# Gated linear attention and a SiLU feed-forward layer on one core: other places for a product block, two masks and a split in the written-out order of a step

## The chip, the cores and the metric

The kernel runs on one core of a Trainium2 chip. Times are device microseconds (us) of one execution. The kernel before was run 14 times: median 681.48 us, from 679.19 to 684.01.

The engines are named as in the profile: PE (TensorE, matrix products) with PEld (its weight loads), DVE (VectorE, elementwise work), ACT (ScalarE, functions from tables), POOL (GpSimd) and SP (SyncE). POOL and SP mostly issue transfers (DMA) here.

## The reference

For each of 4 batches and 8 heads, a state matrix of 48 x 48 complex numbers is carried over 768 positions. At each position it is multiplied by a complex gate, the outer product of k and v is added, and q reads it out. The result, laid out as 3072 tokens of 384 numbers, goes through a feed-forward layer.

```python
mag = np.sqrt(a_re * a_re + a_im * a_im)
scale = np.minimum(mag, 0.999) / (mag + 1e-06)
a_re_n, a_im_n = (a_re * scale, a_im * scale)
...
new_re = ar * S_re - ai * S_im
new_im = ar * S_im + ai * S_re
S_re, S_im = (new_re + kv, new_im)
y[:, :, t] = np.einsum('bhd,bhde->bhe', q[:, :, t], S_re)
...
h = x @ w_in
g = h * (1.0 / (1.0 + np.exp(-h)))
return (g @ w_out).astype(np.float32)
```

## The kernel before, in words

The sequence is cut into chunks of 128 positions: 6 chunks in each of 4 batches are 24 tiles, and two tiles (A and B, of two batches) make a pair p, of which there are 12 (p = 0 to 11). For each pair the kernel does the following.

- *Gates* (`gates_square` to `gates_angle`, lines 304 to 362): from a_re and a_im come l, the logarithm of the gate's size, and th, its angle in turns. ACT does squares, Ln, Exp and Arctan, DVE the sums and products between them. Each change of the set of functions is a table load on ACT (`table`, line 290).
- *Running sums*: th and l are summed over the positions of the chunk by a product with a triangle of ones (`phases`, `sums`). `in_two` (line 372) first splits the input into two parts on DVE. ACT then makes sines and cosines (`trig`, line 410) and exponentials (`decays`).
- *Attention*: DVE multiplies k and q by these (`rotated`) and transposes them in blocks (`turned`); the transfers of tile T on SP and POOL finish the transposition. PE makes the products of q and k (`weights`, line 496), DVE masks them (line 506), PE adds the part from the state (`output`) and makes the next state (`state`).
- *Feed-forward*: `hidden` (line 586) is one eighth of the first product for a pair: two columns of blocks of 256 tokens into the PSUM tile h, followed by SiLU on ACT into the tile g. `result` is one eighth of the second product. From pair 2 on it is done with seven block products for eight (`result_of_halves`, line 647), which needs sums of parts of g. `sums_of` (line 614) makes them on DVE into the tile gs: those of eighth jp+1 are made right behind the matmuls of eighth jp.

The pairs are staggered. After a start in which the pairs 0 to 2 are woven together, a loop over p = 3 to 12 does a *step* each: attention of pair p, feed-forward of pair p-1, and gates of pair p+1 (so gates are made in the steps p = 3 to 10, and the step p = 12 has feed-forward work alone). The order of all instructions in a step is written by hand, in the string `usual` (line 919), and each engine gets its instructions in that order. `step` (line 683) reads it token by token:

- h and r: one eighth of the first and of the second product; the eighths are counted in order, so that the n-th h and the n-th r of a step are called h1 to h8 and r1 to r8 below
- E: exponentials of pair p; kA, qA, kB, qB: `rotated`; tA, tB: `turned`; a0A, a1A, a0B, a1B: `weights` with its mask, for the heads 0 to 3 and 4 to 7; sA, sB: `state`; yA, yB: `output`
- D, L, F, G, th: the gates of pair p+1. D is squares, L the logarithm and what hangs on it, F the inverse of mag + th, G l, the ratio and the arctangent, th the side, the angle and the carried angle
- uA, uB and mA, mB: splits of th and of l; pA, pB: `phases`; lA, lB: `sums`; S: `trig`
- A and X: loads of gates for pair p+2, of k, q, v for pair p+1; c: the angles carried over

Where a token has nothing to do in a step it is left out. In the steps p = 11 and 12 every h and r is followed by `look` (line 722): a load of a part of the weights, and on DVE a smallest value of one that came earlier, for a check at the end.

Buffers that matter here: h has two PSUM buffers (pool `p_h`, line 114), shared by nothing else in the steps; the products of attention, the running sums and the states take turns in two more (pool `p_m`, line 113); gs has two buffers and g four.

Of the kernel before, what the change touches and what calls it, by code (L numbers as in the profile page):

```python
# [60 lines left out]
def kernel(  # L61
# [20 lines left out]
    B, H, S, D = q.shape  # L82
# [43 lines left out]
    A = [dict() for _ in range(NP)]  # L126
    X = {n: dict() for n in range(N)}
# [668 lines left out]
    with tc.manual_schedule(engines={mybir.EngineType.PE}):  # L796
# [104 lines left out]
        for n in (4, 5):  # L901
# [14 lines left out]
        both(trig, 3)  # L916
        startup_psum.close()
        late.append(fast.enter_context(tc.tile_pool(name="o_late", bufs=4, space=PSUM)))
    usual = ("c h E h kA qA h r tA D L kB F qB h r h tB r G h th uA uB A X a0A h a1A r sA h a0B yA "
             "r a1B sB r pA yB pB mA S mB r r lA lB")  # L920
    by_hand.append(True)
    with tc.manual_schedule():
        for p in range(3, NP + 1):
# [179 lines left out]
```

## Time and profile before

| what | value |
|---|---|
| median of 14 runs | 681.48 us |
| profiled execution, its own time | 681.21 us |
| its span, first to last instruction | 679.4 us |
| PE, PEld busy | 645.2, 572.8 us |
| DVE, ACT, POOL busy | 457.1, 345.5, 167.8 us |
| ACT table loads | 64, 1283 ns each |
| SiLU, one eighth | 596 ns |
| mask of `weights` | 685 ns |
| one step of the loop, between the same places of two passes | 52.02 us |

The profile is of one execution. Busy time is the union of an engine's instructions. A row of the timeline gives start and length in us, engine, line, operation, the tiles (out<-in), shapes and how many instructions it merges; in brackets stands how long the engine had been idle and what ended that wait. PE and PEld are one engine seen twice: weight loads run beside the matmul before them, and the ends of matmuls are modelled, so the distance between starts says more than a length.

### The profile page before, as it was taken

What the parts mean: (1) busy time and instruction counts of PE and PEld (TensorE: products, weight loads), DVE (VectorE), ACT (ScalarE), POOL (GpSimd) and SP (SyncE); (2) the same over time, 40 slices, a digit from 0 to 9 for tenths busy, and PEclk for the clock granted to TensorE, in tenths of its full rate; (3) what the DMA queues carried; (4) which work ended last, traced back from release to release, by engine and by line L of the source; (5) the groups of instructions that cost most, each with busy time, mean ns of one, the idle gap of its engine ahead of it and who ended that gap; (6) DMA issues with size and microseconds to landing.
All of it is one profiled execution on the core that took longest, in us unless ns stands there. A gap on an engine that the chain in (4) does not pass through costs nothing. (4 is left out here: it accounts for less than half of the span.)

```text
span 679.4 us, 11283 instructions
## 1 busy us (share of the span) xinstructions
PE 645.2 (95%) x4066; PEld 572.8 (84%) x4066; DVE 457.1 (67%) x979; ACT 345.5 (51%) x526; POOL 167.8 (25%) x256
## 2 busy tenths in 40 slices
PE   5788999999999999999999999999999999998995
PEld 3576777577989989989989989989989989997995
DVE  3786745939775875885784784784785784874532
ACT  7779543665942842752762761771780681510110
POOL 7473201340320320320330230240240240240000
PEclk8799999999999999999999999999999999998998
DMA  9968658281392382293184185184176164577630
GB/s 170 225 134 194 141 141 185 49 134 34 37 143 39 51 137 54 46 137 59 36 130 72 35 127 77 31 120 91 31 110 101 31 96 68 193 162 211 217 114 28
DMA packets 171488, 71.20 MB, mean 105 GB/s; under 512 B 155904, under 2 KB 160000, under 8 KB 171424
## 3 DMA queue, kind: packets, MB, share of 16 engines
q1 hardware_dynamic: 158304, 49.76, 36.8%
q0 software_dynamic: 8768, 15.92, 15.4%
q10 hardware_dynamic: 4352, 4.72, 2.0%
q8 instruction: 34, 0.56, 0.4%
q14 instruction: 30, 0.25, 0.1%
HBM read 48.86 MB, written 4.79 MB: 79 GB/s over the span
## 5 line engine op out<-in xcount | busy, mean ns | idle before, releaser
L591 PE MATMUL h<-xT,w 128*128 128x256 f32 x1152 | 260.9, 380 | 5.8 <-ACT g L295 4.7
L591 PEld LDWEIGHTS h<-xT,w 128*128 128x128 f32 x1152 | 215.9, 190 | 36.7 <-ACT g L295 7.1
L295 ACT ACTIVATE g<-h 128x512 f32<-128x512 f32 x96 | 55.5, 596 | 165.4 <-PE h L591 162.2
L492 POOL DMA_DIRECT2D T<-sq x120 | 78.5, 665 | 69.3 <-issue 59.3
L290 ACT ACT_TABLE_LOAD x64 | 82.1, 1283 | 2.5 <-PEq L1087 1.3
L663 PE MATMUL o<-w,gs 128*128 128x192 f32 x320 | 79.0, 329 | 0.0
L542 POOL DMA_DIRECT2D xT<-y x30 | 15.9, 535 | 216.2 <-ACT y L538 197.3
L506 DVE TENSOR_TENSOR w<-a,upto_r 128x512 f32<-128x512 f32 x48 | 32.0, 685 | 52.6 <-PE a L501 52.6
L663 PE MATMUL o<-w,g 128*128 128x192 f32 x320 | 66.8, 331 | 0.0
L663 PE MATMUL o<-wc,gs 128*128 128x192 f32 x320 | 65.1, 326 | 0.0
L534 ACT COPY xT<-y 128x384 f32<-128x384 f32 x20 | 9.6, 479 | 102.7 <-PE y L528 102.7
L663 PEld LDWEIGHTS o<-w,gs 128*128 128x128 f32 x320 | 56.0, 190 | 1.7 <-DVE gs L620 1.7
L663 PEld LDWEIGHTS o<-w,g 128*128 128x128 f32 x320 | 53.8, 190 | 3.5 <-issue 1.9
L620 DVE TENSOR_TENSOR gs<-g 128x128 f32<-128x128 f32 x160 | 38.9, 284 | 26.0 <-ACT g L295 14.6
L501 PEld LDWEIGHTS a<-T 96*128 96x128 f32 x384 | 49.3, 192 | 5.9 <-issue 2.8
L663 PEld LDWEIGHTS o<-wc,gs 128*128 128x128 f32 x320 | 54.2, 190 | 0.0
L440 POOL DMA_DIRECT2D decs<-ends x48 | 30.5, 642 | 92.3 <-DMA ends<-eq 91.3
L501 PE MATMUL a<-T 96*128 96x128 f32 x384 | 50.4, 276 | 2.7 <-DMA T<-sq 2.3
L633 PE MATMUL o<-w,g 128*128 128x384 f32 x128 | 42.6, 488 | 0.0
L663 PE MATMUL o<-wc,g 128*128 128x192 f32 x160 | 39.1, 326 | 0.0
L633 PEld LDWEIGHTS o<-w,g 128*128 128x128 f32 x128 | 24.2, 190 | 16.1 <-issue 0.2
L525 PE MATMUL y<-w,v 128*64 128x128 f32 x320 | 36.1, 288 | 0.0
(106 smaller groups left out, 953.2 us busy)
## 6 DMA issues: line engine op xcount, KB each, us to landing
T<-sq SPq DMA_DIRECT2D x120, 64.0 KB
T<-sq POOLq DMA_DIRECT2D x120, 64.0 KB, 4.3
raw<-in_moe_w_out_dram SPq DMA_DIRECT2D x16, 384.0 KB
small<-in_moe_w_in_dram SPq DMA_DIRECT2D x16, 384.0 KB
small<-in_moe_w_out_dram SPq DMA_DIRECT2D x16, 384.0 KB
raw<-in_moe_w_in_dram SPq DMA_DIRECT2D x24, 192.0 KB
out_dram<-ot ACTq DMA_DIRECT2D x23, 192.0 KB
q<-in_q_dram SPq DMA_DIRECT2D x18, 192.0 KB
```

The lines of the kernel that those rows point to most:

```text
L290: chain(nc.scalar.preload_act_table_set({"exp": "natural_log_exp_and_others", "trig": "trig_and_small", "silu": "silu_and_others"}[of]))
L295: chain(nc.scalar.activation(out=out, in_=in_, func=func, **kw))
L440: nc.gpsimd.dma_start(out=decs[a * D:(a + 1) * D, n], in_=ends[n].rearrange("(h d) -> d h", d=D))
L492: (nc.gpsimd if a % 2 else nc.sync).dma_start(out=to[ts(b, Q), :, a], in_=sq[ts(a, Q), b])
L501: nc.tensor.matmul(ps[:, h], lhsT=x["kT"][:, hh * HH + h], rhs=x["qT"][:, hh * HH + h], start=True, stop=True)
L506: nc.vector.tensor_tensor(out=x["w", hh], in0=ps, in1=upto.unsqueeze(1).to_broadcast([C, HH, C]), op=ALU.mult)
L525: nc.tensor.matmul(to, lhsT=v_[:, cols], rhs=x["w", h // HH][:, h % HH], start=True, stop=not carried)
L542: (nc.gpsimd if r and n >= EARLY else nc.sync).dma_start(out=xT[64 * r + D:64 * r + 64, dc], in_=y3[64 * r + third * dc:64 * r + third * ( ...
L591: nc.tensor.matmul(ps[:, ji], lhsT=w1[:, dc, ts(jp * 2 + ji, C)], rhs=A[p]["xT"][:, dc], start=(dc == 0), stop=(dc == ND - 1))
L620: nc.vector.tensor_tensor(out=t[:, i], in0=a, in1=b, op=op)
L633: nc.tensor.matmul(A[p]["o"][m].rearrange("p n c -> p (n c)"), lhsT=A[p]["g", jp][:, ji, ts(m, C)], rhs=w2[:, j], start=(j == 0), stop=(j ...
L663: nc.tensor.matmul(o[i], lhsT=a, rhs=b, start=(jp == 0 and i < 4), stop=(final and i in ((5, 3, 6, 2) if p == NP - 1 else (4, 5, 6, 2))))
```

## The change

Two lines of the string `usual` are written differently. h4 and its SiLU move from behind qB to ahead of L; qB and r2 stand between L and F; A, X and the first masked product a0A stand ahead of th, uA and uB; r7 stands ahead of mB. Nothing is added or removed.

```diff
-    usual = ("c h E h kA qA h r tA D L kB F qB h r h tB r G h th uA uB A X a0A h a1A r sA h a0B yA "
-             "r a1B sB r pA yB pB mA S mB r r lA lB")
+    usual = ("c h E h kA qA h r tA D kB h L qB r F h tB r G h A X a0A th uA uB h a1A r sA h a0B yA "
+             "r a1B sB r pA yB pB mA S r mB r lA lB")
```

## The prediction

> **What bounds the kernel now.** I read the page's rows of busy time and slices first, then the costliest groups with their releasers, then one loop pass (step p=7, 376.5 to 428.6 us) row by row.
>
> ```profile
> PE 645.2 (95%) x4066; PEld 572.8 (84%) x4066; DVE 457.1 (67%) x979; ACT 345.5 (51%) x526; POOL 167.8 (25%) x256
> PE   5788999999999999999999999999999999998995
> ...
> L591 PE MATMUL h<-xT,w 128*128 128x256 f32 x1152 | 260.9, 380 | 5.8 <-ACT g L295 4.7
> L591 PEld LDWEIGHTS h<-xT,w 128*128 128x128 f32 x1152 | 215.9, 190 | 36.7 <-ACT g L295 7.1
> ```
>
> TensorE is full in every slice from the fifth to the last but two. What can still be won is idle time of TensorE inside the steps, nothing else. The groups show one repeated hole: the weight loads of the first product (h) wait 7.1 us for a SiLU (g on ACT). In step p=7 the hole looks like this. The rows are "start, length, engine, line, operation"; the last fence shows the two other places that the change touches.
>
> ```profile
> 395.29 1.28 ACT L290 ACT_TABLE_LOAD   x1
> 396.58 1.09 ACT L295 ACTIVATE g<-h 128x512 f32<-128x512 f32 x2
> 397.69 1.28 ACT L290 ACT_TABLE_LOAD   x1
> ```
>
> ```profile
> 391.47 2.51 PEld L591 LDWEIGHTS h<-xT,w 128*128 128x128 f32 x12
> ...
> 396.01 0.35 PEld L663 LDWEIGHTS o<-w,gs 128*128 128x128 f32 x2
> 397.23 2.46 PEld L591 LDWEIGHTS h<-xT,w 128*128 128x128 f32 x12 [0.87 <-ACT g L295]
> ```
>
> I number the blocks of a step in TensorE's order: h1 h2 h3 r1 h4 r2 h5 r3 h6 a0A h7 a1A r4 sA h8 a0B yA r5 a1B sB r6 pA yB pB r7 r8 lA lB. The h tile has two PSUM buffers, so h6 needs the SiLU of h4. Its weight loads began at 386.60, and it was over by 389.6, but that SiLU stands in ACT's order behind L and F, and starts only at 396.58, after F's table load. It is done at 397.17; h6 starts at 397.23.
>
> ```profile
> 406.42 1.51 PEld L574 LDWEIGHTS s<-v,kr 128*96 128x96 f32 x16
> ...
> 426.64 0.30 PEld L663 LDWEIGHTS o<-w,gs 128*128 128x128 f32 x2 [0.21 <-DVE gs L620]
> ```
>
> ```profile
> 405.53 1.28 DVE L506 TENSOR_TENSOR w<-a,upto_r 128x512 f32<-128x512 f32 x2
> ...
> 426.31 0.48 DVE L620 TENSOR_TENSOR gs<-g 128x128 f32<-128x128 f32 x2
> ```
>
> Last block r8 waits 0.21 us for its sums gs, which DVE makes behind both l splits (mB). The masks of a0A and a1A run at 405.53, just ahead of sA, which takes the first mask's buffer.
>
> **What is not touched.** TensorE's order is the same before and after: only ACT and DVE tokens change places around h and r. SP and POOL issue in the same order too: A and X (4 and 6 loads on SP) pass th, uA and uB, which issue no DMA; r7 passes mB, which issues none; S's two stores stay behind tB and the y parts. There are 64 table loads before and after.
>
> **Part 1: h4 ahead of L** (steps p=3 to 10, eight of them, the ones with a next pair of gates). What a hole costs is read from first weight load to first weight load. An h after an r takes 2.54 us there (391.47 to 394.01), an r after an h 2.33. So r3 and h6 without a hole take 4.87; they take 399.71 - 394.01 = 5.70. Loss 0.83 us. The first step has 188.18 to 189.15 idle, 0.97, so 0.93; the other six, at 241, 293, 345, 449, 501 and 553, repeat the 0.87 row's hole. Sum 0.93 + 7 x 0.83 = 6.7 us.
>
> Here a rule of the Trainium skill matters: "Perfetto Trace Analysis", Identifying the Most-Contended Engine, says that matmul busy time misleads because the matmuls are pipelined, and that weight-load busy time is the better measure. By the PE row the holes are worth 4.7 us, by the PEld row 7.1. The block spacing lies between, because after a hole the next block's loads come 0.06 sooner (2.48 for 2.54). I take 6.7, close to what the rule would choose.
>
> What is late next: ACT. The SiLU of h4 now starts when h4 ends. In the step without gates the same wait is visible: h4's loads start at 591.94, SiLU at 594.90, 2.96 later. That gives 386.60 + 2.96 = 389.56 and an end at 390.16. ACT would have begun L's table load at 388.08; now at 390.18, 2.10 later. The skill speaks against the change here: "TensorE: Matmul & The Clock Gate", Architectural detail, calls the ACT and DVE queues strict FIFO, so everything behind that SiLU waits 1.5 us with it. By the rule alone the change pays 2.10 us of ACT per step (8 x 2.10 = 17 us if it reached TensorE). The rows say how much arrives. L and F take 388.08 to 396.57 = 8.49, so they end at 398.67; SiLU of h5 runs 398.68 to 399.28. It is needed by h7, whose loads start at 400.71 - 0.83 = 399.88. Margin 0.60 us, so nothing reaches TensorE. Then trig table, arctan, silu table: SiLU of h6 at 402.7 instead of 402.16, needed by h8 at 407.86 - 0.83 = 407.0.
>
> DVE inside this stretch: qB no longer stands behind F's sum (mag + th, 0.96), which waited for ACT (0.33). Order now: kB from 389.25, qB from 390.8, gs of r2 from 392.3, F's sum from 393.35 (its input, 391.09 before, arrives at 393.19) to 394.3. ACT needs it for F at 393.57 + 2.10 = 395.67, margin 1.4. Transposes of tB start at 394.25, 0.3 earlier, so the T transfers of B are not later. gs of r3 no longer waits for ACT (0.82); gates_l and ratio end at 399.05, just before arctan's new time of 400.6.
>
> T of A is the other guard. a0A now comes at 399.71 - 0.83 = 398.88; the last POOL transfer of T for A landed at 396.83. Margin 2.0; in the first step 190.70 against 188.94.
>
> **Part 2: masks ahead of angles.** The a0A mask (0.69) goes in front of side, angle, carried, uA, uB. It waits for a0A, whose matmuls end at 400.1: DVE idles 399.05 to 400.15, masks to 400.83. Then side to 401.4, the first angle operation when arctan ends (401.42), and from there 405.53 - 400.88 = 4.65 as before, to 406.1; a1A's mask to 406.8, where it ended before (406.81). Alone this saves nothing: sA waited for nobody. It is cover for Part 1: sA now comes at 405.59, and with the old order the first mask would end at about 406.2 plus 0.6 for the later arctan. That would give back 1.2 of 0.83. New position: the buffer is free at 400.83. The second mask is needed by a0B at 409.5, margin 2.7; uA and uB, 0.6 later, by pA at 419.5. Cost 0.
>
> **Part 3: r7 ahead of mB.** mB's four splits become two ahead of gs: gs starts 0.87 earlier (425.44 for 426.31), its first result is there 0.6 before r8 asks. r8 took 2.46 (425.43 to 427.89) where r7 took 2.29: 0.18 us a step, x8 = 1.4. mB then ends about when gs ended, 427.3; lB's loads come at 428.23 - 0.18 = 428.05. Margin 0.7.
>
> **Steps 11 and 12.** Step 11 has no gates; h4 takes its check of the weights (tiny, 0.55 on DVE) ahead of qB. Both stand ahead of tB in either order: 0. The 2.64 us hole ahead of a0B (616.07) stays: its DVE chain hangs on a load that keeps its place on SP. The clock there dips (0.96 granted in 584.1 to 632.8; y took 3.27 for 1.96). Where such a dip falls can move with the rest: 0 to -1.4, I take 0. Step 12 is the same program.
>
> **Sum.** 681.21 (profiled execution: span 679.4 and 1.8 around it) - 6.7 - 1.4 = 673.1. That execution lies 0.27 under the median of 681.48; so 673.3 as a median. 0.2% (1.4 us) is about what this measurement can tell from no change.
>
> **Rivals.**
> *Part 3 gives nothing* (the rest as above): for it, r8's wait is the smallest of the terms and a wait can go to another input; against it, the row names gs. 681.48 - 6.7 = 674.8. Chance 0.10.
> *A new wait eats part*: SiLU of h5 is the tightest margin, 0.60. Were it 0.3 to 0.9 later than that, 8 x 0.3 to 0.9 = 2.4 to 7 comes back: 676 to 680, middle 677. For: ACT has no idle left between 388 and 399. Against: every ACT length is taken from the same rows. Chance 0.11.
> *It does not do what it says*: h6 waits for something else, and ACT merely ends last. SiLU ends 0.06 before h6 starts in the row, and gaps repeat to 0.01 us, so hardly. 681.5, within 0.2%. Chance 0.04.
> *Slower: ACT's FIFO wait reaches h7.* Place: h7's weight loads. Every us that SiLU of h5 is later than 399.88 costs 8 us in all; it is slower than before once that SiLU is 0.60 + 1.01 = 1.6 us behind my 399.28. For that F's sum on DVE must come about 3 us late (1.4 margin + 1.6), for instance if gs of r2 or qB ahead of it meets a wait that the old order hid. At 2.5 us late: 8 x (2.5 - 1.61) = +7, 688.6. For: DVE now has qB and gs in front of that sum. Against: both have all inputs by 386. Chance 0.09.
>
> The main case holds 0.66. Faster 0.66 + 0.10 + 0.11 = 0.87, same 0.04, slower 0.09. Range: low end 673.3 - 1.4 (clock dip) - 0.6 (spread of medians) = 671.3; high end the middle of the partial case, 677.0. It leaves out the upper half of that case, the same and slower cases, under 0.2.
>
> **What would show it.** h6 without a releaser row, and h6's first weight load directly behind r3's last; a step of 51.0 us for 52.02; SiLU of h4 apart from that of h5, with about 1.5 us of ACT idle ahead of it released by PE h; first mask 5 us earlier than the second; no gs wait in r8. I am wrong if h7, sA or lB gains a wait on ACT or DVE, if a0A waits for T, or if the hole of step 11 grows.

## The result, and the profile after

| | before | after |
|---|---|---|
| median | 681.55 us (47 runs) | 675.88 us (10 runs, 671.01 to 679.02) |
| profiled execution, its own time | 681.21 us | 677.81 us |
| its span | 679.4 us | 676.1 us |
| one step of the loop, p = 4 to 9 | 52.02 us | 51.00 us |

The changed kernel takes 0.9898 of the time of the one before, 95% interval 0.9873 to 0.9923. That is the ratio of the two means (675.06 and 682.02 us), about 7 us; the medians are 5.7 us apart. The forecast was 673.3 us with 671.3 to 677.0 around it. Direction and mechanism were right. The median lies 2.6 us above the forecast, and the steps themselves are not where those microseconds are.

The page after: busy time, slices of PE, and the two groups that showed the hole at h.

```profile
PE 645.2 (95%) x4066; PEld 575.0 (85%) x4066; DVE 454.9 (67%) x979; ACT 345.4 (51%) x526; POOL 163.9 (24%) x256
...
L591 PE MATMUL h<-xT,w 128*128 128x256 f32 x1152 | 262.2, 382 | 1.1 <-ACT xT L565 1.1
L591 PEld LDWEIGHTS h<-xT,w 128*128 128x128 f32 x1152 | 217.8, 191 | 30.4 <-ACT xT L565 1.8
```

No h waits for a SiLU any more: 4.7 us of releasers on PE and 7.1 on PEld are gone, and what stays is from the start of the kernel. Now the step p = 7, which begins about 0.43 us later than in the profile before (h4's loads at 387.03 for 386.60). PEld's rows of r3, h6 and a0A, of sA, and of r8 with the sums behind it:

```profile
396.44 0.35 PEld L663 LDWEIGHTS o<-w,gs 128*128 128x128 f32 x2
396.76 2.51 PEld L591 LDWEIGHTS h<-xT,w 128*128 128x128 f32 x12
399.30 1.08 PEld L501 LDWEIGHTS a<-T 96*128 96x128 f32 x8
...
406.01 1.52 PEld L574 LDWEIGHTS s<-v,kr 128*96 128x96 f32 x16
...
425.02 0.68 PEld L663 LDWEIGHTS o<-w,g 128*128 128x128 f32 x4
425.67 0.35 PEld L663 LDWEIGHTS o<-wc,g 128*128 128x128 f32 x2
425.99 0.35 PEld L663 LDWEIGHTS o<-w,gs 128*128 128x128 f32 x2
...
427.29 0.70 PEld L390 LDWEIGHTS L<-l_parts,half_r 128*128 128x128 f32 x4
```

h6 follows r3 without a gap and without a releaser; r8 takes 427.29 - 425.02 = 2.27 us, as r7 does. ACT has the wait instead:

```profile
387.64 0.84 ACT L295 ACTIVATE th<-re 128x768 f32<-128x768 f32 x1
389.99 0.60 ACT L295 ACTIVATE g<-h 128x512 f32<-128x512 f32 x1 [1.50 <-PE h L591]
390.60 1.28 ACT L290 ACT_TABLE_LOAD   x1
...
399.11 0.60 ACT L295 ACTIVATE g<-h 128x512 f32<-128x512 f32 x1
```

The SiLU of h4 stands alone, 1.50 us of idle ACT ahead of it. That of h5 ends at 399.71, and h7's weight loads start at 400.30: 0.59 us to spare. DVE's two masks of A are apart:

```profile
400.61 0.69 DVE L506 TENSOR_TENSOR w<-a,upto_r 128x512 f32<-128x512 f32 x1 [1.62 <-PE a L501]
...
406.54 0.68 DVE L506 TENSOR_TENSOR w<-a,upto_r 128x512 f32<-128x512 f32 x1
```

**Where the time went.** I divided both profiled executions at the same pieces of work: the first weight load of a second-product block, the first of step 3, and that of lA in step 10.

| stretch | before | after | difference |
|---|---|---|---|
| start, to the first block of the second product | 60.99 | 65.60 | +4.61 |
| from there to r1 of step 3 | 115.10 | 115.11 | +0.01 |
| r1 of step 3 to lA of step 10 | 405.11 | 396.81 | -8.30 |
| from there to the end | 98.19 | 98.56 | +0.37 |

The sum is -3.3, which is the difference of the spans. The loop gave 8.3 us. The start, whose instructions the change does not touch, took 4.6 us longer in this execution; the experiments come back to that.

### The profile page after: what moved, and what is told of

The parts are those of the page before. It is cut to its first block, busy times and chain, and to the rows that moved or that the text cites. A ratio compares the mean times of both kernels' runs of the same rounds, so it can differ in the third digit from the quotient of the medians.

```text
span 676.1 us, 11274 instructions
## 1 busy us (share of the span) xinstructions
PE 645.2 (95%) x4066; PEld 575.0 (85%) x4066; DVE 454.9 (67%) x979; ACT 345.4 (51%) x526; POOL 163.9 (24%) x256
```

## The experiments

For each kernel the step is the distance between the first weight loads of lA in two successive steps, from its own profile; it repeats to 0.02 us within a profile. "Loop" is the stretch from the first block of the second product to lA of step 10: 520.21 us before, 511.92 after.

**One part at a time.** The four kernels of this group are compared with one set of runs of the kernel before (median 681.53).

`e1_h4_only`, h4 moved together with qB and r2, masks and mB where they were:

```diff
-... qA h r tA D L kB F qB h r h tB r G h th uA uB A X a0A h a1A ...
+... qA h r tA D kB h L qB r F h tB r G h th uA uB A X a0A h a1A ...
```

> h4 ahead of L with qB and r2 between L and F, but the masks behind the angles and mB ahead of r7 as before. Theory (the masks are the cover of the first part): h6 no longer waits, 0.83 us a step, but the first mask, which stood 0.2 us ahead of sA, now comes about 0.6 us later while sA is 0.83 earlier, so sA waits about 1.2 us for DVE w in each of eight steps. A step takes 52.02 - 0.83 + 1.2 = 52.4, and the kernel 681.5 + 3 = 684.5: slower than before. Rival (the hole at h6 is all there is): sA doesn't wait, 674.8.

Measured: 683.65 us, ratio 1.0022 (1.0002 to 1.0042); step 52.37; loop 521.69. PEld around sA, then the DVE rows that it waits for:

```profile
406.17 0.35 PEld L663 LDWEIGHTS o<-w,gs 128*128 128x128 f32 x2
407.75 1.43 PEld L574 LDWEIGHTS s<-v,kr 128*96 128x96 f32 x16 [1.24 <-DVE w L506]
```

```profile
402.38 0.96 DVE L360 SCALAR_TENSOR_TENSOR mag<-re,mag 128x768 f32<-128x768 f32 x1 [2.43 <-ACT mag L295]
...
407.02 1.28 DVE L506 TENSOR_TENSOR w<-a,upto_r 128x512 f32<-128x512 f32 x2
```

The hole at h6 is gone, and sA has one of 1.24 us in its place: the angles wait 2.43 us for the later arctangent, and both masks stand behind them. The part that carries the gain is, without the masks, a little slower than the kernel before. The sum expected 3 us; it is 1.5 in the loop, since step 10 has no sA (its step is 48.42 for 49.26) and I had counted eight waits where there are seven.

`e2_masks_only`:

```diff
-... r G h th uA uB A X a0A h a1A ...
+... r G h A X a0A th uA uB h a1A ...
```

> Only A, X and the first mask ahead of the angles, the rest as before. Theory: sA waited for nobody, so nothing is gained: step 52.02, 681.5. The second mask ends about 0.7 us later than before and that is hidden too. Rival (the early mask itself is worth something): faster by 1 us or more.

Measured: 681.93, ratio 1.0003 (0.9989 to 1.0018); step 52.03. The early mask alone is worth nothing. It is cover for the first part. (The loads A and X move with the mask here, as they do in the whole change.)

`e3_r7_only`:

```diff
-... yB pB mA S mB r r lA lB
+... yB pB mA S r mB r lA lB
```

> Only r7 ahead of mB, the rest as before. Theory: the wait of r8 for gs goes, 0.19 us in eight steps: step 51.83, in all 1.5 us, 680.0; lB does not wait. Rival: the gain of the whole change is larger than its parts and this part gives nothing, 681.5.

Measured: 680.68, ratio 0.9985 (0.9966 to 1.0003); step 51.84; loop 518.82, 1.39 less. The interval of the ratio includes 1, so the times alone do not show this gain; the step shows the 0.18 us, and r8's row has no releaser.

`e4_h4_masks`: both moves of the first group, mB ahead of both r as before.

```diff
-... tA D L kB F qB h r h tB r G h th uA uB A X a0A h a1A ...
+... tA D kB h L qB r F h tB r G h A X a0A th uA uB h a1A ...
```

> h4 ahead of L and the masks ahead of the angles, but mB ahead of r7 as before. Theory: step 52.02 - 0.83 = 51.19, in all 6.7 us, 674.8; the wait of r8 for gs stays at 0.21 us. Rival (the parts help each other): step 51.00 as in the whole change, so that r7's place is worth nothing.

Measured: 674.34, ratio 0.990 (0.987 to 0.993); step 51.19; loop 513.43, 6.78 less. r8 waits for gs as before:

```profile
422.39 0.30 PEld L663 LDWEIGHTS o<-w,gs 128*128 128x128 f32 x2 [0.22 <-DVE gs L620]
```

So the loop's 8.29 us are 6.78 from h4 with its cover and 1.39 from r7; the two hardly touch each other.

**What protects the gain.** These are compared with another set of runs of the kernel before (median 680.99).

`e5_no_swap`, qB and r2 behind F:

```diff
-... tA D kB h L qB r F h tB ...
+... tA D kB h L F qB r h tB ...
```

> The changed kernel, but with qB and r2 behind F (L F qB r h) instead of between L and F. Theory (qB and r2 are in the gap so that DVE does not stand still until ACT has the first Exp): F's sum stands ahead of qB and waits for ACT some 2 us, qB and gs of r2 come about 2 us later, gs of r3's block is late by about 0.5 us, so a step takes 51.5: 8 x 0.5 = 4 us above the changed kernel, 679. Rival (the place of qB and r2 does not matter): step 51.00, 675.

Measured: 680.51, ratio 0.9968 (0.9943 to 0.9992); step 51.80. PEld in r3, and DVE:

```profile
397.28 0.35 PEld L663 LDWEIGHTS o<-wc,g 128*128 128x128 f32 x2
398.46 0.30 PEld L663 LDWEIGHTS o<-w,gs 128*128 128x128 f32 x2 [0.83 <-DVE gs L620]
```

```profile
395.79 0.96 DVE L332 TENSOR_TENSOR mag<-mag,th 128x768 f32<-128x768 f32 x1 [2.42 <-ACT mag L295]
...
398.12 0.48 DVE L620 TENSOR_TENSOR gs<-g 128x128 f32<-128x128 f32 x2
```

F's sum stands in front of DVE's queue for 2.42 us until ACT has the Exp that the SiLU of h4 made later. Behind it wait qB and the sums that r3 needs. I had expected 0.5 us at r3; it is 0.83. Most of the gain is lost again, 0.80 of 1.02 us a step, by the place of one token pair.

`e6_abs_in_d` and `e7_abs_in_f` put the same two operations on ACT, at two places of the changed kernel, once ahead of the SiLU of h4 and once behind it:

```diff
         special(th, re, AF.Abs)
+        for _ in range(2 if p > 3 else 0):
+            special(th, re, AF.Abs)
```

```diff
         special(mag, mag, AF.Exp, scale=-1.0)
+        for _ in range(2 if p > 3 else 0):
+            special(th, re, AF.Abs)
```

> The changed kernel with D's last operation, the absolute value of re (0.73 to 0.86 us on ACT), done three times instead of once in the steps p = 3 to 10; same output. Theory: the SiLU of h4 leaves ACT idle for 1.5 us in front of it, and the two more operations fill it; what is left over, at most 0.25 us, lies within the 0.59 us by which the SiLU of h5 is ahead of h7. Step 51.00, no change from the changed kernel. Rival (ACT is full between D and G, and every us there costs): step 52.5, 12 us slower.

> The changed kernel with the same two more operations at the end of F instead, behind the SiLU of h4 and ahead of that of h5; same output. Theory (margin of 0.59 us at h7): the SiLU of h5 comes 1.5 to 1.7 us later, h7 waits 0.9 to 1.1 us for ACT g in each of eight steps: step 51.9 to 52.1, 7 to 9 us above the changed kernel. Rival (ACT is busy half of the time, so 1.6 us hide anywhere): step 51.00.

Measured: in D 671.32, ratio 0.986 (0.9822 to 0.9899), step 51.00; in F 681.83, ratio 1.0005 (0.9985 to 1.0026), step 52.07. The rows of ACT in D, then ACT and PEld in F:

```profile
382.99 2.60 ACT L295 ACTIVATE th<-re 128x768 f32<-128x768 f32 x3
385.49 0.58 ACT L295 ACTIVATE g<-h 128x512 f32<-128x512 f32 x1
```

```profile
397.20 1.70 ACT L295 ACTIVATE th<-re 128x768 f32<-128x768 f32 x2
398.93 1.28 ACT L290 ACT_TABLE_LOAD   x1
400.22 0.60 ACT L295 ACTIVATE g<-h 128x512 f32<-128x512 f32 x1
```

```profile
398.80 1.08 PEld L503 LDWEIGHTS a<-T 96*128 96x128 f32 x8
400.87 1.16 PEld L593 LDWEIGHTS h<-xT,w 128*128 128x128 f32 x6 [0.99 <-ACT g L295]
```

In D the 1.7 us fill the idle time and cost nothing. In F they move the SiLU of h5 by 1.6 us; 0.59 of it is slack, and h7 waits 0.99. Eight such waits undo the whole change: the loop takes 512.10 us with the operations in D and 520.45 with them in F. ACT is busy 51% of the span, and that says nothing on what its time costs: that depends on which side of one SiLU the work lies.

**The hole of step 11.** `e8_looks_behind` is the changed kernel with three of the checks of the weights put off:

```diff
             if x in "hr" and p + 1 >= NP:
+                if p + 1 == NP and "tA" in seen and "tB" not in seen:
+                    held.append(x)
+                    continue
                 look()
+                if held and "sB" in seen:
+                    held.pop()
+                    look()
```

> The changed kernel with another order of the checks of the weights in step 11: those behind h4, r2 and h5 are made up for behind r6, r7 and r8. Theory: the hole of 2.5 us ahead of a0B is T of B, late because its transposes on DVE stand behind a check that waits for a load; without it the hole goes, and with it the 3.4 us at half clock that follow it: 2.5 + 1.5 = 4 us faster than the changed kernel, 671.5. Rival: T of B is late because of its transfers, the hole stays, and the kernel is as fast as the changed one.

Measured: 668.57 (668.42 to 669.83), ratio 0.9805 (0.9775 to 0.9836); step 51.00; from lA of step 10 to the end 94.24 us for 98.56. Changed kernel, DVE ahead of tB's transposes in step 11, and PE at a0B:

```profile
600.83 0.55 DVE L247 TENSOR_REDUCE tiny<-small 128x1 f32<-128x384 f32 x1 [4.66 <-DMA small<-in_moe_w_in_dram]
601.30 0.97 DVE L487 STREAM_TRANSPOSE sq<-kr 128x768 f32<-128x768 f32 x1
```

```profile
612.63 1.13 PE L501 MATMUL a<-T 96*128 96x128 f32 x8 [2.48 <-DMA T<-sq]
```

And PEld with the checks put off:

```profile
603.57 2.51 PEld L592 LDWEIGHTS h<-xT,w 128*128 128x128 f32 x12
606.11 1.08 PEld L502 LDWEIGHTS a<-T 96*128 96x128 f32 x8
```

A check on DVE waited 4.66 us for a load; the transposes for T of B stood behind it. With the checks put off, the transposes come earlier and a0B follows h8 directly. The transfers of T of B took about as long as ever (last landing on POOL 8.3 us after the last transpose, 8.9 in the changed kernel), so it was their late start, not their length, that made the hole. The granted clock, the share of TensorE's full clock that the profile records, is 1.00 in the 12 us around that place (605 to 617 us), where it was 0.86 in the changed kernel (609 to 621). The 4.3 us are both together: the profiles with the hole but without the lower clock behind it (below) put the hole at about 2.3 and the clock at about 2. Every run of this kernel lies below every run of the changed kernel (671.01 at the least); `e6_abs_in_d`, timed beside it, is 2.75 us slower.

**The start.** The profiles have two lengths of it. The first block of the second product began between 60.6 and 62.0 us in seven of the ten profiles so far, and at 65.60, 65.81 and 64.54 us in three (the changed kernel, e3, e5), though this part of the program is the same in all. In those three the granted clock falls to half between 44 and 47 us and stays there for 7 to 10 us (in e2 for 3.4, with a first block at 61.95). Just ahead of that PE waits at the state product of tile 0: 1.33 to 1.63 us in those three, at most 1.13 in the other seven. `after_again` is the changed kernel with no edit; `e9_warm` has 14 idle products (matrix products whose result nobody uses) more, at the place where TensorE waits at 44 us; `e10_looks_warm` has these and the checks put off. The runs of the kernel before beside them have a median of 682.08.

```diff
         turned(1, [2, 3])
+        warm(14)
         state(0)
```

> The changed kernel once more, unchanged. Theory (its steps are 51.00 us in every execution, and what moves its time is the start): times in groups, some at 671 to 673 and some at 675 to 679, step 51.00 in the profile whatever the start does. Rival (the steps vary from run to run): another step length.

> The changed kernel with 14 idle products (about 1.5 us of TensorE at full clock) where TensorE waits about 0.8 to 1.6 us for a mask at 44 us, ahead of the state of tile 0. Theory: in the executions that start late, that wait is what brings half clock from 44 to 55 us, which costs 4 to 5 us; with the products there the clock stays at full there, the first block of the second product comes at 61 us in the profile, and the higher group of times goes: median 672, from 671 to 673. Rival (the late start has another cause, such as the first loads): the groups stay, median 675.

> The same 14 idle products and the checks of step 11 behind r6, r7 and r8. Theory: both gains, 668 with a spread of 2 us. Rival: no better than with the checks moved alone, because that one's executions were mostly of the early start already.

Measured: again 674.48 (671.26 to 677.10), ratio 0.9863 (0.9835 to 0.9891), step 51.00, late start (65.15 us) in the profile; with the products 673.44 (671.60 to 674.97), ratio 0.9866 (0.9841 to 0.9891), first block at 60.91; with both 669.14 (668.42 to 669.53), ratio 0.9796 (0.9771 to 0.9821). The stretches of the start, in the columns "window, its length, busy us of PE, PEld, DVE, ACT, POOL with counts, granted clock, DMA share, GB/s", first of the changed kernel again, then with the products:

```profile
40.80:44.20 3.40, 1.97 (x19) 1.78 (x17) 3.40 (x7) 3.37 (x6) 0.70 (x1) 0.99 0.37 124
44.20:47.60 3.40, 3.40 (x27) 3.31 (x27) 1.80 (x5) 0.78 (x2) 3.40 (x6) 0.50 0.75 158
```

```profile
40.80:44.20 3.40, 3.40 (x25) 2.64 (x21) 3.40 (x7) 3.00 (x7) 3.04 (x5) 1.00 0.59 187
44.20:47.60 3.40, 3.17 (x42) 2.76 (x40) 2.82 (x6) 2.42 (x4) 3.00 (x5) 1.00 0.94 185
```

Each run also has its mean granted clock. In the 16 runs of the changed kernel that the two medians rest on, every one with 0.982 or less took 675.3 us or more, and every one with 0.984 or more took 674.7 or less. With the products all six are at 0.984 to 0.989 and under 675: the upper group is absent. As the changed kernel beside it had that group in two runs of six only, this could still be chance; the profiles are the better evidence. That group is probably also why e4 and e6, with one such run in six each, have lower medians than the changed kernel though their steps are no shorter.

But the median was to be 672, and 671.6 to 675.0 is no narrower than the lower group, so something else moves the rest. The profiles show one such thing at the other end. In all kernels that keep the checks where they were, the hole ahead of a0B is there, but the clock falls behind it in some executions only. From lA of step 10 to the end takes 98.1 to 99.3 us in the six profiles in which it falls (before, after, `after_again`, e1, e2, e4) and 96.3 to 97.4 in the five in which it does not (e3, e5, e6, e7, e9): about 2 us. e8 and e10, without the hole, take 94.24 and 93.79 there, and their runs spread over 1.4 and 1.1 us, those of e9 over 3.4. That this dip explains e9's spread is likely, not shown run by run.

e10 met its rival: it is no better than e8, whose six runs all have 0.984 or more without any products. Whether that was chance in e8 is open.

## Why the prediction was right, and where it was off

**Part 1, h4 ahead of L: right.** The step that carried it was the block spacing, 0.83 us a hole, 6.7 us in all; e4 shows 6.78 in the loop. The two busy rows would have said 4.7 or 7.1; the page cited there speaks of nearness to the roofline, not of what one hole is worth. The price on ACT came as worked out too: SiLU of h4 at 1.50 us of waiting (1.5 predicted), SiLU of h5 0.59 us ahead of h7 (0.60). The strict order of ACT's queue, which spoke against the change, is as hard as the rule cited there says: e7 shows that behind this SiLU 0.59 us are free and the rest goes to TensorE at full price.

**Part 2, masks: right.** 0 by itself (e2), and without it sA gives back more than h6 won (e1: 1.24 us waited, 1.2 predicted). T of A stayed a guard only: its last POOL transfer landed at 397.42, a0A's loads came at 399.30.

**Part 3, r7: right.** 1.4 us; e3 shows 1.39. mB ended at 426.91, lB's loads came at 427.63, the margin of 0.7 that was given.

**Steps 11 and 12: right as far as they went.** The hole ahead of a0B stayed (2.85 us on PEld for 2.64), in this profile with its dip of the clock. Its slice of the page is the one exception to "full in every slice": it reads 8. The dip was put at 0 to 1.4 us and taken as 0; it is worth about 2, in some executions.

**The sum: right in the loop, off in the median.** -8.1 was forecast, -8.3 measured between the same two pieces of work. With the start of the profile before, the profiled execution would have taken 677.81 - 4.61 = 673.2 us; 673.1 was forecast for it. What the sum left out was a term that the change does not contain: it took the start of one profiled execution (60.99 us) as the start of every execution; the later start costs 3.5 to 5 us against that one. For the kernel before this did little harm: of its 63 runs beside the experiments, 10 have a mean clock of 0.982 or less. Of the ten runs behind the median of 675.88 six have it, and all six lie above 675. The other four, 671.0 to 673.1, lie just under the forecast. Why so many of these ten are of the low clock is open: `after_again`, the same kernel, has two of six. That the median still fell inside the range is luck in this respect: the upper end, 677.0, stood for waits that did not come. That the start explains the whole 2.6 us is argued from clocks of single runs, not shown for each: only profiled executions show their start.

**The rivals.** No new wait, no loss of part 3, and a hole that was what its row said. The slower rival named the right place, h7, but not the nearest danger to a version of this change: e5 and e1 show that the DVE's order decides earlier, with qB and r2 or with the masks in the wrong place.

## What to carry to other kernels

Where one engine is full, read a hole from block start to block start, move the instruction that ends it, and then ask for each engine what is now late behind the moved one: here the move lost without the masks (e1), lost most of its gain without the place of qB and r2 (e5), and paid with both. The share of busy time of an engine with a strict order does not say whether its time is free; the slack up to the next waiting instruction does, and it can be measured by putting a known operation on either side. A comparison of a few microseconds should be made between the same two pieces of work in both profiles, so that a start which varies by itself does not enter.

## What the runs showed of the hardware that was not expected

TensorE's granted clock fell to half for 10.2 us (44.1 to 54.4 in `after_again`) behind a stretch of 3.4 us in which it was busy for 1.97 us; in the kernel before, the wait at the same place left it 2.64 us busy in such a stretch (43.4 to 46.8), and the clock did not fall. The longest single gap there was 1.63 us (changed kernel). The Trainium skill, "TensorE: Matmul & The Clock Gate", HAM oscillation, tells to avoid idle gaps of more than about 3.4 us; here a stretch that was partly idle was enough, in some executions and not in others. With 14 idle products in that stretch the clock stayed at full in both profiles that have them.

The same happened at the other end, behind the hole ahead of a0B in the changed kernel (2.85 us on PEld). The columns are those of the start:

```profile
611.01:614.42 3.41, 1.79 (x21) 1.70 (x23) 0.55 (x1) 0.00 (x0) 0.00 (x0) 1.00 0.93 301
614.42:617.83 3.41, 3.41 (x27) 3.05 (x24) 2.03 (x6) 0.65 (x2) 0.00 (x0) 0.50 0.83 293
```

The length of the hole does not decide it: e7's is longer (3.12 us), and the clock stayed at full. In every profile all changes of the granted clock lie whole multiples of 3.41 us apart, as if on a grid (44.39, 54.63, 614.42 and 617.83 us in the changed kernel). The place of the grid differs: counted from the first instruction it begins at 0.02 us there, at 2.42 in the kernel before and at 1.10 in e7. In e7 the hole lies across an edge of it, with 1.81 and 2.26 us of PE busy on the two sides. In the six profiles in which the clock fell, PE was busy for 0.78 to 1.79 us of the stretch ahead of the fall; in the five in which it did not, the least was 1.71 (e6) to 2.06. Part 1 of the skill's page calls the window in which activity is watched free-running, and the grid agrees with that. No single busy share can be read from these runs as the limit: at the start the clock fell behind 2.31 us (e2) and not behind 2.28 (e1).
